# A fused RWKV-6 attention and GELU MLP on one core: the end of the first token tile put in another order, with two packing transfers in place of six

## The chip, the cores and the metric

The kernel runs on one NeuronCore of a Trainium2 chip. The metric is the device time of one execution in microseconds (us); the time shown is the median of the runs. Names of engines: PE is the matrix engine (PEld its weight loads), DVE the vector engine, ACT the scalar engine, POOL the general engine, SP the engine that here only issues transfers. ACT issues a few transfers as well.

## The reference

Four batch rows, 8 heads, 768 steps, head size 48. The recurrence of each head, followed by a two-layer MLP with exact GELU on all 3072 tokens:

```python
for t in range(S):
    cur = np.einsum('bhd,bhe->bhde', u[None] * kt, vt)
    y[:, :, t] = np.einsum('bhd,bhde->bhe', rt, state + cur)
    state = wt[:, :, :, None] * state + np.einsum('bhd,bhe->bhde', kt, vt)
x = attn_out.transpose(0, 2, 1, 3).reshape(3072, 384)
h = x @ w_in                                   # 384 x 2048
out = 0.5 * h * (1 + erf(h / sqrt(2))) @ w_out # 2048 x 384
```

The two weight matrices come as 64-bit floats and are made into 32-bit floats on the chip.

## The kernel before

**Tiles.** The 3072 tokens are cut into 8 tiles of 384 (half of one batch row). Tile x first goes through `attention(x, unit)`, which leaves the 384 x 384 activations transposed in `xT`, and then through `mlp(x)`, which reads `xT`. While PE works on the MLP of one tile, the attention of the next is woven into it. Only the first tile has no MLP to be woven into: its attention is all there is to do.

**Order.** Each piece of work is a Python generator, and the string `PLAN[x]` names, letter by letter, which generator goes on to its next `yield`. The order of the instructions on each engine is therefore written out by hand; engines run their own instructions strictly in that order and wait for each other through semaphores. For tile 0 the letters are: "." unit 0 and "s" unit 1 (the two halves of the heads, which go through `attention` one after the other, offset by a step), "f" the attention of tile 1, "c" the conversion of weights, "l" the loads of weights and of tile 1, "w" the values of tile 1, "x" the function `warm`. What is left of ".slxw" after the string is run out at its end.

**Attention of the first tile.** Inside a chunk of 64 steps the products of r and k are formed by levels (1, 2, 4, 8, 16, 32). For each level PE multiplies (`products`, L480), a part of the result goes to `a_sb`, and DVE multiplies r and k by the decays of the level (`update`, L522, or both at once, L533). At level 32 only the update of k is done at once; the one of r is kept in the list `last_r`, and the copies of the products to `a_sb` in `last_rows`. In this text the last products of the two units are called the last bursts. Then follow, for each unit:
- k is transposed on PE (`kt_ps`, L720, 6 transposes in two banks; there are just two such banks, tag "mm"), ACT copies it to `kx` (L727);
- the copies of `last_rows` (L738), on ACT for unit 1 and on DVE for unit 0; then r is updated by `last_r`;
- `kv_ps` (L764): the products of k and v for each chunk;
- `inside()` (L805): `y_ps`, what comes from inside the chunks;
- `chain_states` (L784, then 10 dependent instructions L779): the states of the chunks, one after the other, on DVE;
- `fences()` (L815, L817): DVE reads one element of `y_ps`, after which PE adds the states' share to it (L847);
- the output goes from `y_ps` to `xT`. A head has 48 rows and a column of `xT` has place for 64 in each half, so three of the four pairs of heads fill rows 0 to 47 of the halves (L854, L870), and the last pair is copied to `ysb` (L873) and laid into the free 16 rows of the three columns by transfers (L877), the packing transfers. For tile 0 three of these six go out from SP and three from ACT, for the other tiles all six from SP.

`x_rows` permutes the rows of `w_in` on the host to fit this layout.

**After it.** `mlp(0)` starts with `h_ps` (L1238): for each of 16 column blocks f of `w_in` three matmuls, one for each column j of `xT`. Before it stand the first products of tile 1 (L480), three matmuls on zeros (`keep_warm`, L253), and behind its first block the products of tile 1 that read ru = u * r (`kx`, made by ACT, L429).

**Weights.** A weight piece is 128 x 768 values in 64 bits. `prepare` makes two 32-bit parts of it by three ACT instructions (L361, L362, L364), `finish` puts them together on DVE (L373, L377). The pieces are prepared two ahead (`HALFWAY`), so the third piece, number 2, is prepared while piece 0 is finished. Loads of the first pieces and of tile 1 wait for a one-column memset on DVE (L191, L232), which sets when SP may issue them.

Of the kernel before, what the change touches and what calls it, by code (L numbers as in the profile page):

```python
# [22 lines left out]
G = 64  # L23
D = 48
# [12 lines left out]
NC_SP = 8  # L37
HALFWAY = 2
PLAN = {
    0: ".lls.....sslsc.lsslll.sl.sls..sl.lscsl..sss.lscs.lscs.s.ssssclll..s...sss..cs...sw.ccff",  # L40
    1: (
        ".cswc.ccc.cccss.lc.ccscs..cc.cs.cclwcsc.ccssc.c.cccsccc..ssccc.c.lcls.cc.ccsc.w.clwscclccc"
        ".c.swcw.ss.ccs.lcsc..cwcccslccslff..w..fw.wfs..f..flffffffww"
# [36 lines left out]
def kernel(  # L80
# [25 lines left out]
    nc = tc.nc  # L106
# [5 lines left out]
    NJ = DM // 128  # L112
# [183 lines left out]
    for i, h in enumerate(QUARTERS[:1]):  # L296
        for a in range(3):
            w_q = (3 - a) * C // 4
            z = q_ints[1 if a == 0 else 2]
# [35 lines left out]
    def conversion():  # L335

        i = converted[0]
        if i >= len(pieces):
            return
        converted[0] += 1  # L340

        prepare(i + HALFWAY)
        yield
        if wide:
            yield from finish(pieces[i][0], raws[i], *halfway[i])
        for _ in weight_in(i + 3):
            pass
# [5 lines left out]
    def prepare(upto):  # L353
        if not wide:
            return
        for i in range(len(halfway), min(upto, len(pieces))):
            words = raws[i].bitcast(U32).rearrange("p (a b) -> p a b", b=2)
            lo, hi = words[:, :, 0], words[:, :, 1]
            f = cv.tile([128, PIECE], U32, name="f")
            e = cv.tile([128, PIECE], U32, name="e")  # L360
            nc.scalar.activation(out=f.bitcast(F32), in_=hi.bitcast(F32), func=AF.Abs, scale=2.0 ** -112)  # L361
            nc.scalar.activation(out=e.bitcast(F32), in_=lo, func=AF.Identity, scale=2.0 ** -51, bias=two)  # L362
            sign = e.bitcast(F16).rearrange("p (a b) -> p a b", b=2)[:, :, 1]
            nc.scalar.activation(out=sign, in_=hi.bitcast(F32), func=AF.Copy, scale=2.0 ** -100)  # L364
            halfway.append((f, e))
# [15 lines left out]
    def attention(x, unit):  # L381
# [16 lines left out]
        xT = xT_of[x]  # L398
# [307 lines left out]
        last_r, last_rows = [], []  # L706
# [3 lines left out]
        if x < 2:  # L710
            kts = []
            for b in range(np_):
                if x == 0:
                    kt_ps = [ps.tile([128, BANK], F32, name="kt_ps", tag="mm", bufs=2) for _ in range(2)]
                else:
                    kt_ps = pair("kt_ps")
                    kt_ps = [kt_ps[:, z] for z in range(2)] + [kt_ps]
                for i in range(NI):
                    o = (i % N3) * 128
                    nc.tensor.transpose(kt_ps[i // N3][:, o:o + 128], k[:, (b * NI + i) * 128:(b * NI + i + 1) * 128], ident)  # L720
                if x == 0:
                    yield
                kt = kx[:, parts[b] * Q * T:(parts[b] + 1) * Q * T].rearrange("p (i g d) -> p i g d", g=2, d=G)
                kt2 = kt.rearrange("p (b i) g d -> p b (i g d)", b=2)
                if x == 0:
                    for z in range(2):
                        nc.scalar.copy(out=kt2[:, z], in_=kt_ps[z][:, 0:N3 * 128])  # L727
                else:
                    nc.scalar.copy(out=kt2, in_=kt_ps[2][:, :, 0:N3 * 128])
                kts.append(kt)  # L730

            if x == 0:
                yield
                for ah, d in last_rows:
                    for p in range(2):
                        rows = slice(p * 64, p * 64 + C // 2)
                        copy = nc.scalar.copy if unit else nc.vector.tensor_copy
                        copy(out=ah[rows, :, :, 0], in_=d[rows, :, :, 0])  # L738
                yield
                for z in last_r:  # L740
                    z()

            def k_t(b, i, p, g):
                return kts[b][half[p], i, g, :]
        else:

            for z in range(4):
                nc.scalar.copy(out=block_of_kt(z, z), in_=kb[z * 32:(z + 1) * 32, z])

            def k_t(b, i, p, g):  # L750
                return kt_q[half[p], g, b * NI + i]
# [23 lines left out]
        def chain_states(steps):  # L775
            for c in steps:
                if c or not first:
                    for q in range(qs):
                        nc.vector.scalar_tensor_tensor(out=stq[:, q, c], in0=stq[:, q, c - 1] if c else b4[:, q, NC - 1],  # L779
                                                       scalar=totq[:, q, c:c + 1], in1=kvs[q // Q][:, q % Q, c // 2, c % 2],  # L780
                                                       op0=ALU.mult, op1=ALU.add)
                else:
                    for b in range(np_):
                        nc.vector.tensor_copy(out=stq[:, b * Q:(b + 1) * Q, c], in_=kvs[b][:, :, 0, 0])  # L784
# [34 lines left out]
        if x == 0:  # L819

            inside()
            yield
            chain_states(range(NC - 1 + int(first)))
            yield
            fences()
            yield
        else:
            for c in range(0, NC, 2):
                chain_states(range(c, min(c + 2, NC - 1 + int(first))))
                if x > 1 and c + 2 < NC:  # L830
                    yield
            yield
            inside()
            fences()
            yield
# [23 lines left out]
        for b in reversed(range(np_)):  # L859
            for q in reversed(range(Q)):  # L860
                which = parts[b] * Q + q
                if x == 0 and which == NP - 2:

                    yield
                y = ys[b][1][:, :, q * N3 * C:(q + 1) * N3 * C].rearrange("p c (i t) -> p c i t", t=C)
                if which < NJ:
                    for z in range(2):
                        s = slice(z * G, z * G + D)
                        copy = nc.vector.tensor_copy if x == 0 else nc.scalar.copy
                        copy(out=xT[s, which, :].rearrange("p (i c t) -> p c i t", c=2, t=C), in_=y[s])  # L870
                    continue
                ysb = wk.tile([128, T], F32, name="ysb", bufs=1)
                nc.scalar.copy(out=ysb.rearrange("p (i c t) -> p c i t", c=2, t=C), in_=y)  # L873
                for z in range(2):
                    for j in range(NJ):
                        e = z * G + j * (G - D)
                        (nc.scalar if x == 0 and z * NJ + j > 2 else nc.sync).dma_start(out=xT[z * G + D:(z + 1) * G, j, :], in_=ysb[e:e + G - D, :])  # L877
        yield


# [500 lines left out]
    second = load_second(nc.sync)  # L1381

    def weights():
        prepare(1)
        yield
        while converted[0] < len(pieces):
            yield from conversion()
            yield

    def next_v():  # L1390
        load_v(1, nc.sync)
        yield

    def warm():
        for _ in range(1):
            keep_warm(3, True)
            yield

    def masks_and_sums():
        yield from make_quarter_masks()  # L1400
# [4 lines left out]
    for x in range(NX):  # L1405
        if x == 2:
            homes()
        following = attention(x + 1, 0) if x + 1 < NX else iter(())
        if x == 0:
            streams = {  # L1410
                ".": units[0], "s": units[1], "f": following, "c": pieces_of_w, "w": next_v(), "x": warm(),
                "l": chain(weight_in(0, True), islice(second, 5), weight_in(1, True), weight_in(2, True), second),
            }
        else:
            streams = {
                ".": mlp(x - 1), "s": slots, "f": following,
                "l": load(x + 1, nc.sync),
                "x": sums_of_x15(x) if x == NX - 1 else sums_of_x(x) if x > 1 else iter(()),
                "w": masks_and_sums() if x == 1 else chain(first_sum(), h_sums()) if x == 2 else sums_of_w15() if x == NX - 1 else iter(()),
                "c": pieces_of_w if x == 1 else iter(()),  # L1420
            }
        for c in PLAN[x]:
            next(streams[c], None)
        for c in ".slxw" if x == 0 else ".slxwc":
            while next(streams[c], streams) is not streams:
                pass
        slots = following
        if x == 1:
            fewer_pairs()
# [4 lines left out]
def x_rows(n_pairs):  # L1434

    rows = []
    for j in range(n_pairs - 1):
        for z in range(2):
            for p in range(G):
                q, e = (j, p) if p < D else (n_pairs - 1, j * (G - D) + p - D)  # L1440
                rows.append((2 * q + (z ^ q // Q % 2)) * D + e)
    return rows

# [48 lines left out]
```

## Time and profile before

| | |
|---|---|
| median of three runs | 591.1 us (587.8, 591.1, 591.87) |
| the profiled execution's own time | 593.53 us |
| its span, first to last instruction | 591.7 us |
| around the span | 1.8 us |
| mean granted PE clock | 0.997 |
| DVE busy, ACT busy | 463 us (78%), 276 us (47%) |
| PE busy from 0 to 50 us | 38.4 of 50 us |
| PE busy from 50 to 200 us | 150 of 150 us |

The profile shows one execution. A timeline line has the start in us, the duration, the engine, the line of the kernel, the operation with output and input, the number of instructions, and in brackets how long the engine stood idle before it and what ended that. A 32-bit matmul is recorded as two instructions. A q behind an engine's name means the engine's issuing side: "SPq L877" is SP issuing a transfer, "DMA xT<-ysb" the transfer itself until it has landed.

### The profile page before, as it was taken

What the parts mean: (1) busy time and instruction counts of PE and PEld (TensorE: products, weight loads), DVE (VectorE), ACT (ScalarE), POOL (GpSimd) and SP (SyncE); (2) the same over time, 40 slices, a digit from 0 to 9 for tenths busy, and PEclk for the clock granted to TensorE, in tenths of its full rate; (3) what the DMA queues carried; (4) which work ended last, traced back from release to release, by engine and by line L of the source; (5) the groups of instructions that cost most, each with busy time, mean ns of one, the idle gap of its engine ahead of it and who ended that gap; (6) DMA issues with size and microseconds to landing.
All of it is one profiled execution on the core that took longest, in us unless ns stands there. A gap on an engine that the chain in (4) does not pass through costs nothing.

```text
span 591.7 us, 17422 instructions
## 1 busy us (share of the span) xinstructions
PE 574.6 (97%) x7509; PEld 509.4 (86%) x7509; DVE 462.9 (78%) x907; ACT 276.0 (47%) x640; POOL 8.0 (1%) x21
## 2 busy tenths in 40 slices
PE   6789999999999999999999999999999999999998
PEld 3566666766799999999998999999999999989997
DVE  5879767988969986787859987688768998985532
ACT  2267889323612558046461468235561465523400
POOL 3100000000000000000000000000000000000000
PEclk9999999999999999999999999999999999999999
DMA  6549671020142311241022310420015200210000
GB/s 237 192 155 320 220 260 56 31 91 1 26 143 78 90 38 31 81 125 38 0 57 86 125 37 16 100 89 33 2 29 166 73 2 2 41 39 8 1 14 34
DMA packets 51004, 46.80 MB, mean 79 GB/s; under 512 B 31728, under 2 KB 36080, under 8 KB 50928
## 3 DMA queue, kind: packets, MB, share of 16 engines
q1 hardware_dynamic: 50832, 45.62, 25.3%
q8 instruction: 59, 0.97, 0.7%
q14 instruction: 17, 0.14, 0.1%
q10 hardware_dynamic: 96, 0.07, 0.1%
HBM read 36.24 MB, written 4.72 MB: 69 GB/s over the span
## 4 chain that ended last, share of the span: by engine, by line
PE 83%; DVE 8%; DMA 4%; SPq 3%; issue 1%; ACT 0%; DVEq 0%
PE o_ps L1252 25%; PE h_ps L1026 15%; PE u_ps L1026 12%; PE h_ps L1238 11%; PE d L619 4%; PE d L480 4%; PE o_ps L1332 4%; SPq L562 2%; PE c_ps L1026 2%; DVE st L779 2%; DMA rkw<-in_rkw_dram 2%; PE y_ps L805 2%; PE y_ps L847 2%; PE kv_ps L764 1%; DMA rkw<-kx 1%
## 5 line engine op out<-in xcount | busy, mean ns | idle before, releaser
L1026 PE MATMUL h_ps<-xT,w_in_sb 128*128 128x192 f32 x408 | 81.2, 330 | 0.1
L1026 PEld LDWEIGHTS h_ps<-xT,w_in_sb 128*128 128x128 f32 x408 | 67.8, 190 | 3.1 <-ACT g L1058 1.2
L1238 PE MATMUL h_ps<-xT,w_in_sb 128*128 128x384 f32 x192 | 64.4, 490 | 0.2 <-DMA xT<-ysb 0.2
L1238 PEld LDWEIGHTS h_ps<-xT,w_in_sb 128*128 128x128 f32 x192 | 35.8, 190 | 24.4 <-issue 0.8
L1252 PE MATMUL o_ps<-w_out_sb,g 128*128 128x192 f32 x224 | 39.5, 326 | 0.0
L1252 PEld LDWEIGHTS o_ps<-w_out_sb,g 128*128 128x128 f32 x224 | 36.9, 190 | 0.3
L480 PEld LDWEIGHTS d<-rkw 64*64 64x64 f32 x1152 | 21.2, 148 | 16.0 <-issue 11.2
L635 ACT COPY a_sb<-d 32x256 f32<-32x256 f32 (+8 forms) x90 | 32.6, 363 | 4.6 <-PE d L619 3.1
L1252 PE MATMUL o_ps<-w_out_sb,f 128*128 128x192 f32 x176 | 31.6, 329 | 0.0
L1252 PE MATMUL o_ps<-t,g 128*128 128x192 f32 x176 | 31.4, 329 | 0.0
L1252 PE MATMUL o_ps<-w_out_sb,e 128*128 128x192 f32 x176 | 31.4, 329 | 0.0
L1252 PE MATMUL o_ps<-t,e 128*128 128x192 f32 x176 | 31.2, 328 | 0.0
L1252 PE MATMUL o_ps<-t,s 128*128 128x192 f32 x176 | 30.9, 327 | 0.0
L480 PE MATMUL d<-rkw 64*64 64x64 f32 (+1 forms) x1152 | 23.8, 236 | 6.7 <-DMA rkw<-in_rkw_dram 3.5
L652 DVE COPY_PREDICATED a_sb<-quarter,d 128x480 f32<-128x480 uint8 (+5 forms) x54 | 23.2, 438 | 8.6 <-PE d L619 7.3
L779 DVE SCALAR_TENSOR_TENSOR st<-st,tot_sb,kv_ps 128x48 f32<-128x48 f32 x160 | 29.0, 257 | 1.0 <-PE kv_ps L764 0.8
L1026 PE MATMUL u_ps<-s,w_in_sb 128*128 128x192 f32 x160 | 29.5, 327 | 0.0
L1252 PEld LDWEIGHTS o_ps<-t,g 128*128 128x128 f32 x176 | 28.7, 190 | 0.4
L1252 PEld LDWEIGHTS o_ps<-w_out_sb,e 128*128 128x128 f32 x176 | 28.7, 190 | 0.3
L1252 PEld LDWEIGHTS o_ps<-w_out_sb,f 128*128 128x128 f32 x176 | 28.7, 190 | 0.3
L1252 PEld LDWEIGHTS o_ps<-t,e 128*128 128x128 f32 x176 | 28.8, 190 | 0.2
L1252 PEld LDWEIGHTS o_ps<-t,s 128*128 128x128 f32 x176 | 28.9, 190 | 0.1
(236 smaller groups left out, 1170.8 us busy)
## 6 DMA issues: line engine op xcount, KB each, us to landing
rkw<-in_rkw_dram SPq DMA_DIRECT2D x54, 256.0 KB, 4.1
raw<-in_w_out_dram SPq DMA_DIRECT2D x8, 768.0 KB, 5.0
v_in<-in_v_dram SPq DMA_DIRECT2D x8, 584.0 KB, 4.6
raw<-in_w_in_dram SPq DMA_DIRECT2D x5, 768.0 KB, 6.8
out_dram<-o_sb SPq DMA_DIRECT2D x20, 192.0 KB, 2.0
rkw<-kx SPq DMA_DIRECT2D x72, 48.0 KB, 2.0
rkw<-in_rkw_dram SPq DMA_DIRECT2D x6, 384.0 KB, 5.2
raw<-in_w_in_dram SPq DMA_DIRECT2D x9, 256.0 KB, 5.1
```

The source lines that it names most:

```text
L480: nc.tensor.matmul(d[half[p], g, n * width:(n + 1) * width], lhsT=kc[half[g], b, i, p], rhs=right(half[g], b, i, p), start=True, stop=True)
L562: dma.dma_start(out=block_of_kt(dst, src), in_=kb[src * 32:(src + 1) * 32, dst])
L619: nc.tensor.matmul(o[half[p], i * 3 * C // 2:(i + 1) * 3 * C // 2], lhsT=kc[half[g], n // NI, n % NI, p], rhs=rx[half[g], 2 * n + p], star ...
L635: nc.scalar.copy(out=at[z, g, first:behind, (a + 1) * h:], in_=d[z, :, :, to] if g == slice(None) else d[z, :, to])
L652: nc.vector.copy_predicated(out=an[:, :, :, :, (a + 1) * h:], mask=mask.to_broadcast(data.shape), data=data)
L779: nc.vector.scalar_tensor_tensor(out=stq[:, q, c], in0=stq[:, q, c - 1] if c else b4[:, q, NC - 1], scalar=totq[:, q, c:c + 1], in1=kvs[q ...
L805: nc.tensor.matmul(y[p][half[g ^ swap(b)], i * C:(i + 1) * C], lhsT=vs(b, i, g)[half[p]], rhs=at[half[p], g, b * NI + i, :], start=(i == 0 ...
L847: nc.tensor.matmul(ys[b][0][c % 2][half[g ^ swap(b)], i * C:(i + 1) * C], lhsT=src[half[g], o:o + G], rhs=rc[half[g], b, i, c % 2], start= ...
L1026: nc.tensor.matmul(o, lhsT=lhsT, rhs=rhs, start=start, stop=True, skip_group_check=True)
L1238: nc.tensor.matmul(h_ps, lhsT=w_in_sb[:, f // FI, j, f % FI * 128:(f % FI + 1) * 128], rhs=xT[:, j, :], start=(j == 0), stop=(j == NJ - 1))
L1252: nc.tensor.matmul(o, lhsT=lhs(j), rhs=rhs(j), start=start and j == 0, stop=(j == HF - 1), skip_group_check=True)
L1332: nc.tensor.matmul(o, lhsT=block(i, f // HF, f % HF), rhs=w_out_sb[:, f, :], start=(f == 0), stop=(f == NF - 1))
```

## The change

1. The string of tile 0 is changed in its second half. In the order of the instructions this puts the last bursts of both units next to each other, before the transposes of either; unit 0's transposes come right after unit 1's, and both `kv_ps` before either `y_ps`. The last instruction that finishes weight piece 0 (L377) comes two steps earlier on DVE, and the last third of piece 2's load goes out after the whole of piece 3's instead of before it.
2. `last_r` is run after `inside()`, ahead of `chain_states`, instead of before `kv_ps`.
3. The copies of `last_rows` change engines: DVE for unit 1, ACT for unit 0.
4. `prepare` has a yield before the third ACT instruction of piece 2; in the order of the instructions, this one comes after the copies of `y_ps` to `xT`.
5. The packing transfers of each half become one: two transfers of 16 x 3 x 384 values instead of six of 16 x 384. For tile 0 one goes out from SP and one from ACT. `x_rows` is changed to fit.
6. `warm` and its three matmuls are gone.

```diff
-    0: ".lls.....sslsc.lsslll.sl.sls..sl.lscsl..sss.lscs.lscs.s.ssssclll..s...sss..cs...sw.ccff",
+    0: ".lls.....sslsc.lsslll.sl.sls..sl.lscsl..sss.lscscc.lss.s...ss..s.llls.csssss....sw.cccff",
...
-        prepare(i + HALFWAY)
+        yield from prepare(i + HALFWAY)
...
             nc.scalar.activation(out=e.bitcast(F32), in_=lo, func=AF.Identity, scale=2.0 ** -51, bias=two)
+            if i == HALFWAY:
+                yield
...
-                        copy = nc.scalar.copy if unit else nc.vector.tensor_copy
+                        copy = nc.vector.tensor_copy if unit else nc.scalar.copy
                         copy(out=ah[rows, :, :, 0], in_=d[rows, :, :, 0])
-                yield
-                for z in last_r:
-                    z()
...
             inside()
+            yield
+            for z in last_r:
+                z()
             yield
             chain_states(range(NC - 1 + int(first)))
...
                 for z in range(2):
-                    for j in range(NJ):
-                        e = z * G + j * (G - D)
-                        (nc.scalar if x == 0 and z * NJ + j > 2 else nc.sync).dma_start(out=xT[z * G + D:(z + 1) * G, j, :], in_=ysb[e:e + G - D, :])
+                    (nc.scalar if x == 0 and z else nc.sync).dma_start(
+                        out=xT[z * G + D:(z + 1) * G, :, :].rearrange("p j t -> p (j t)"), in_=ysb[z * G:z * G + D, :])
...
-    def warm():
-        for _ in range(1):
-            keep_warm(3, True)
-            yield
...
-                q, e = (j, p) if p < D else (n_pairs - 1, j * (G - D) + p - D)
+                q, e = (j, p) if p < D else (n_pairs - 1, (p - D) * (n_pairs - 1) + j)
```

More of the change, by code (lines that the diff above doesn't have):

```diff
@@ L1383, in weights @@
     def weights():
-        prepare(1)
+        yield from prepare(1)
         yield
@@ L1410 @@
             streams = {
-                ".": units[0], "s": units[1], "f": following, "c": pieces_of_w, "w": next_v(), "x": warm(),
+                ".": units[0], "s": units[1], "f": following, "c": pieces_of_w, "w": next_v(),
                 "l": chain(weight_in(0, True), islice(second, 5), weight_in(1, True), weight_in(2, True), second),
@@ L1423 @@
             next(streams[c], None)
-        for c in ".slxw" if x == 0 else ".slxwc":
+        for c in ".slw" if x == 0 else ".slxwc":
             while next(streams[c], streams) is not streams:
```

## The prediction

> **What bounds the kernel.** I read the page's engine totals first: PE is busy 97% of the span. Then PE's waits after the first tile, from 48 us to the end:
>
> ```profile
> PE kv_ps L764 <- DMA rkw<-kx: 1.3, 2, 1.0
> PE y_ps L805 <- DVE st L779: 1.0, 3, 0.4
> PE y_ps L847 <- issue: 0.2, 1, 0.2
> PE h_ps L1238 <- DMA xT<-ysb: 0.2, 1, 0.2
> ```
>
> Each line gives total us, times, longest. In 540 us PE waits 2.7 us: from the first MLP on, PE sets the end, and the time moves by what the start of mlp(0) moves. So the chain of waits from 25 to 50 us is the view that matters (start, us, what):
>
> ```profile
> 33.49 0.57 DVE rkw L522
> ...
> 34.20 0.85 PE kt_ps L720 x6
> ...
> 37.00 0.56 DVE a_sb L738
> 37.55 0.03 issue
> 37.59 0.27 DVE st L784
> 37.85 0.03 issue
> 37.88 1.84 DVE st L779 x10
> 39.72 0.07 DVE fence L817
> ...
> 41.95 0.47 ACT ysb L873
> 42.42 0.02 issue
> 42.44 0.61 SPq L877
> ...
> 43.82 4.16 DMA xT<-ysb
> 47.97 0.14 issue
> 48.11 0.88 PE h_ps L1238 x2
> ```
>
> Unit 1's state chain on DVE could start at 37.59 only because DVE was copying unit 0's rows (L738); then come the chain, the states' share on PE, ysb, three transfers one behind the other on SP, and the third lands 4.16 us after its issue. PE's timeline shows how nearly it kept up with that:
>
> ```profile
> 42.90 1.38 PE L847 MATMUL y_ps<-rkw,st 64*64 64x64 f32 x40 [0.32 <-DVE fence L815]
> 44.12 1.73 PE L480 MATMUL d<-rkw 64*64 64x32 f32 x96
> 45.78 0.82 PE L253 MATMUL warm<-zeros 128*128 128x512 bf16 x3
> 46.44 1.45 PE L1238 MATMUL h_ps<-xT,w_in_sb 128*128 128x384 f32 x4
> 48.11 0.88 PE L1238 MATMUL h_ps<-xT,w_in_sb 128*128 128x384 f32 x2 [0.21 <-DMA xT<-ysb]
> ```
>
> My mark is the end of that first block, where tile 1's next products start: 48.92.
>
> **Bursts, transposes, r.** Up to unit 1's last burst (32.50) PE's order is the same. Unit 0's burst follows it: its r and k are ready at 33.07 (L533, 32.11 + 0.96), so it runs 33.24 to 34.17, in what was PE's 0.77 us wait for the update of k. Unit 1's transposes still start at 34.20. Unit 0's now come right behind, but there are two banks, so they wait for ACT's copies of unit 1's (34.75 to 35.61): a new wait. Behind it on PE stands unit 1's kv_ps, and DVE's chain waits for that: transposes end about 36.1, kv_ps runs 36.08 to 36.95 (before: to 36.59, so 0.36 later). DVE meanwhile does both updates of k (to 34.8), the copies of unit 1's rows (1.11, to 35.9) and r (0.56, to 36.6), all ahead of 36.95; L377 (0.95) has moved into DVE's idle 1.35 us before 32.11 and costs nothing, and the memsets behind it release their loads about 0.6 to 0.9 us later. Those loads have room: the last of them were moved by 39.4 (the transfer engines fall to 0.06 busy at 40), the first products of tile 1 want theirs at 43.5. So the chain starts at 37.0 instead of 37.59: 0.58 us gained.
>
> From there the same steps follow in the same order: chain and fence (2.2), states' share of unit 1, inside of unit 0, fence, states' share of unit 0, tile 1's products. Unit 1's `inside` (37.75 to 38.7, behind ACT's new row copies) is done before its fence at 39.2, as is r. PE's unexplained 0.40 us inside L847 (at 40.17, "issue") sits at the same count of instructions, and I keep it; nearest other such pauses are 0.71 and 1.76 us, so this is -0.4 to +1.4, and I take 0. Everything moves by 0.58: ysb ends at 41.85, tile 1's products end where h_ps can start, at 45.2.
>
> **Warm-up removed.** 46.44 - 45.78 = 0.66 us of PE's path.
>
> **Transfers.** SP and ACT issue one each at 41.9. Before, the first column needed two transfers and only the third column waited; now the first matmul waits for both. Needed at 45.2, they may take 3.3 us. What is shown for old ones, for tile 0:
>
> ```profile
> DMA to landing us min/median/max: 1.9/2.0/4.2
> ```
>
> The first on SP took 2.1, with an empty queue before it, as now. The two new ones carry 147 KB; the first old pair's 48 KB moved in some 0.35 us (the bytes seen from 43.6 to 43.9), so three times as much adds 0.7: landing after 2.8 us (an estimate from these rows), at 44.7, with 0.5 us to spare. The upper bound is the row of the third old one, 4.16, which had the load of v on its heels, issued 0.88 us after it; now that load follows again, some 0.7 us behind. I take 2.8: nothing stands in front of it on SP (idle 5.6 us), and the load's bytes came about 1.2 us after its issue, so at 43.8 to 44.0, as the packing ends. On that queue the later transfers (v, two weight pieces, tile 2) all go 2 us earlier.
>
> [...]
>
> The old wait for the third column is gone: six matmul records at 0.33 us (7.94 us for 24) are 1.98, so the block would have ended at 48.6 without it, against 48.92: 0.35 us with warm-up's overlap. Sum: 45.2 + 1.98 = 47.2 against 48.92, or -1.7 (0.58 + 0.66 + 0.35, and 0.1 of rounding).
>
> **Third weight piece in two parts.** L364 (1.07) now stands behind the copies to xT, ahead of ACT's L429, on which the products after the first block wait. ACT's copies start at 43.85, L364 at 44.75, the four L429 end at 46.3, 46.8, 47.35 and 47.9 (0.53 each); their products want them from 47.2 in steps of 0.4: no wait, 0.3 us if all starts faster. Before, the piece was ready at 40.82 and ACT idled 1.11 before ysb, so taking it off that path gains nothing. Its DVE half was wanted at 50.5 and PE's at 56.4: room.
>
> **Later tiles.** In each, four issues on SP fall away (0.59 each); only h_ps and DVE's sums wait for them, and PE showed no such wait. From 0 to -1.3 (all waits of kv_ps for transfers), and I take 0. Pieces of w_in and w_out come with at least 3 us of room (piece 1 ready at 49.5, used at 52.4; the last of w_out ready at 107.5, used at 111.2), and ACT, nearly full at 90 to 100 us, last waited for PE at 81.1, so it moves with PE.
>
> **Rivals.** (1) The packing lands behind the load of v, 4.16 us after issue, at 46.1: the block ends at 48.1, -0.85, so 590.25. For it: that very row, and its equal order. Against: the first transfer's 2.1. (2) The clock: PE had 1.94 us of work in 24 to 28 us, and then this came:
>
> ```profile
> 28.00:31.00 3.00, 2.79 (x62) 1.84 (x66) 2.54 (x7) 2.85 (x4) 0.00 (x0) 0.55 0.20 52
> ```
>
> The third number from the right is the granted clock, 0.55. If leaving out the three matmuls brought that on again for 3 us at the start of h_ps, 3 x 0.45 = 1.35 us would be lost: -0.35, so 590.75. Against: from 39 to 41 us PE did 0.76 us of work in 2 us and was granted 1.00. [...] (3) Slower: the packing transfers get caught in the burst of loads that now starts 2 us earlier. A load of tile 2 issued at 47.9 took 7.5 us to land; at that price h_ps starts at 41.9 + 7.5 = 49.4 and the block ends at 51.4, +2.5, so 593.6. It decides from a landing of 5.0 us (41.9 + 5.0 + 1.98 = 48.9). For it: transfers up to 394 GB/s from 50 us; against: all of those loads are issued after the packing. (4) PE's gain is given back because weights or loads stay where they are: 591.1. Against: the room above. (5) SP's emptier queue also ends the 1.3 us waits of kv_ps: -3.0, so 588.1. Against: other issues stand between, for tiles 2 and 3.
>
> **The numbers.** Forecast -1.7: the profiled execution of 593.53 (span 591.7 and 1.8 around it) would be 591.8, span 590.0. The median of the runs is 2.4 below that execution, and from it I get 589.4. Chances: forecast 0.50, (1) 0.22, (2) 0.06, (3) 0.08, (4) 0.08, (5) 0.06. The range goes from (5) to (2), 588.1 to 590.75, and 1.0 us beyond on both sides, because three runs that lie 4.1 us apart do not fix a median better (an estimate): 587.1 to 591.75. About what a measurement can tell from no change is 1%, 5.9 us: no case reaches it. What is left is scatter of the runs: faster 0.03, slower 0.04, within 0.93.
>
> **What would show it.** Right: the first L784 near 37.0, h_ps starting about 45.2 with no wait, the products after it near 47.2, and PE without waits after that. Rival (1): h_ps starts near 46.1 with a wait for xT<-ysb. Rival (2): a granted clock under 1.00 between 44 and 50. Rival (3): a wait there of over 3.5 us. The prediction is wrong if PE shows new waits after 48 us, or if the first chain does not start earlier.

## The result, and the profile after

| | before | changed |
|---|---|---|
| median | 590.67 us (587.8 to 591.87, 8 runs) | 594.91 us (592.64 to 599.19, 8 runs) |
| ratio, 95% interval | 1 | 1.0081, 1.0057 to 1.0106 |
| profiled execution, its span | 593.53, 591.7 us | 597.55, 595.8 us |
| mean granted PE clock | 0.997 | 0.991 |

The kernel became 0.8% slower, about 4 us, where 1.7 us less was forecast; 594.91 lies outside the range of 587.1 to 591.75. PE is still busy 97% of the span.

PE's waits from 48 us to the end, of the changed kernel (total us, times, longest):

```profile
PE d L482 <- issue: 1.9, 1, 1.9
PE y_ps L804 <- DVE st L778: 1.1, 3, 0.4
PE h_ps L1027 <- DVE o_sb L1376: 0.7, 1, 0.7
PE kv_ps L763 <- DMA rkw<-kx: 0.7, 2, 0.5
```

The wait for `xT<-ysb` is gone, as intended. At the top stands something new: 1.9 us in one piece, put down to "issue", which means that nothing the profile shows held PE. PE's timeline shows where:

```profile
39.32 1.98 PE L849 MATMUL y_ps<-rkw,st 64*64 64x64 f32 x33 [1.83 <-issue]
...
43.20 2.16 PE L849 MATMUL y_ps<-rkw,st 64*64 64x64 f32 x38 [0.32 <-DVE fence L814]
45.15 0.25 PE L482 MATMUL d<-rkw 64*64 64x32 f32 x2
...
46.80 2.17 PE L1239 MATMUL h_ps<-xT,w_in_sb 128*128 128x384 f32 x6
48.90 0.68 PE L482 MATMUL d<-kx,rkw 64*64 64x64 f32 x27
51.50 1.87 PE L482 MATMUL d<-kx,rkw 64*64 64x64 f32 x69 [1.92 <-issue]
53.30 9.00 PE L1239 MATMUL h_ps<-xT,w_in_sb 128*128 128x384 f32 x24
62.23 1.60 PE L482 MATMUL d<-rkw 64*64 64x32 f32 x96
```

The same place before:

```profile
48.92 1.63 PE L480 MATMUL d<-kx,rkw 64*64 64x64 f32 x96
50.48 8.01 PE L1238 MATMUL h_ps<-xT,w_in_sb 128*128 128x384 f32 x24
58.42 1.60 PE L480 MATMUL d<-rkw 64*64 64x32 f32 x96
```

The first block of h_ps starts without a wait right behind tile 1's products. Then PE stops after 27 of 96 records of the products that read kx, and no wait for an operand is shown. The 24 records of h_ps after it take 9.00 us (before: 8.01), and the last 38 of L849 2.16 us (before: 1.38 for 40). The windows say why (width, then busy us of PE, PEld, DVE, ACT and POOL, then granted clock, share of the transfer engines, GB/s):

```profile
40.00:44.00 4.00, 3.68 (x93) 3.50 (x91) 1.06 (x4) 0.48 (x1) 0.00 (x0) 0.50 0.12 33
...
48.00:52.00 4.00, 2.08 (x62) 1.26 (x64) 3.66 (x12) 3.42 (x8) 0.00 (x0) 0.99 1.05 398
52.00:56.00 4.00, 4.00 (x56) 2.73 (x49) 3.77 (x4) 1.57 (x2) 0.00 (x0) 0.58 1.01 372
```

Over the 4 us after each stop the granted clock was 0.50 and 0.58; before, it was 1.00 from 40 to 56 us. And while PE stands at 50 us, the transfer engines are full (a share of 1.05 from 48 to 52 us).

From tile 1's first products to the end of the 24 h_ps, before took 14.30 us (44.12 to 58.42) and the changed kernel 17.08 (45.15 to 62.23). The 2.78 us between are: the block of h_ps starts sooner and waits less, -1.05; the stop, +1.92; the rest of those products, most of them on the slow clock, +0.92; h_ps on the slow clock, +0.99. From the end of those 24 h_ps to the end of the span it is 533.3 us before and 533.6 in the changed kernel (531.6 to 533.6 in all profiles of ordinary length, of both kernels and of the experiments). So all but 0.3 of the 4.1 us between the two spans arises in the first 62 us.

The remaining 1.03 us lie ahead of tile 1's first products, and there the two executions are no even match. At unit 1's last burst the changed kernel stood 3.16 us ahead (29.34 against 32.50), because before had shortly ahead of it stopped for 1.76 us and run on a clock of 0.55. It lost that lead and 1.03 us more up to 45.15, behind its stop of 1.83 us inside L849 (0.40 in L847 before) and the slow clock after it.

### The profile page after: what moved, and what is told of

Its sections match the earlier page's. It is cut to its first block, busy times and chain, and to the rows that moved or that the text cites. A ratio compares the mean times of both kernels' runs of the same rounds, so it can differ in the third digit from the quotient of the medians.

```text
span 595.8 us, 17357 instructions
## 1 busy us (share of the span) xinstructions
PE 577.1 (97%) x7506; PEld 511.9 (86%) x7506; DVE 462.7 (78%) x907; ACT 275.7 (46%) x640; POOL 8.0 (1%) x21
## 5 line engine op out<-in xcount | busy, mean ns | idle before, releaser
L1242 ACT ACTIVATE g<-h_ps 128x256 f32<-128x256 f32 (+1 forms) x32 | 13.9, 434 | 31.1 <-PE h_ps L1239 30.5
```

The source lines that it names most:

```text
L1242: nc.scalar.activation(out=gs[group][:, f % FG, 0:t], in_=h_ps[:, 0:t], func=AF.Gelu)
```

## What the stops are: a theory and its rivals

The page's list of DMA queues has a row that I had not used (packets, MB, share):

```profile
q1 hardware_dynamic: 50352, 45.62, 25.0%
q8 instruction: 59, 0.97, 0.7%
```

One packet of q8 is 0.97 MB / 59 = 16 KB. PE has 7506 matmuls and 7506 weight loads; in 59 pieces that is 254 instructions each, some 64 bytes apiece (estimates from these rows). And the stops on PE stand at multiples of 128 matmul records: between the two shown, 38 of L849, 48 of L804, 40 of L849, 96 of the tile's products, 6 of h_ps and 27 make 255, two pieces less one record. From this I take it that PE's own program comes in pieces of 128 matmuls and their weight loads during the run, over the transfer engines that carry the data (q1 25.0% of them, q8 0.7%).

When a piece moved is seen by cutting the run into slices of 0.4 us and looking for the packet. For the piece that the products of kx need, from 48.8 to 49.2 us of the changed kernel:

```profile
q1 hardware_dynamic: 83, 0.16, 104.2%
q8 instruction: 1, 0.02, 15.7%
```

Before, the same piece moved between 45.2 and 45.6 us, 1.1 to 1.5 us after PE had entered the piece ahead of it (44.12), beside little else:

```profile
q1 hardware_dynamic: 29, 0.02, 23.6%
q8 instruction: 1, 0.02, 20.7%
```

Now it moved 3.7 us or more after that point (45.15). What came in between is on SP's timeline (start, time of issue):

```profile
42.16 0.69 SPq L877 DMA_DIRECT2D xT<-ysb  x1
42.98 0.49 SPq L184 DMA_DIRECT2D v_in<-in_v_dram  x1
43.52 1.01 SPq L228 DMA_DIRECT2D raw<-in_w_in_dram  x2
44.78 0.53 SPq L204 DMA_DIRECT2D rkw<-in_rkw_dram  x1
45.41 2.55 SPq L228 DMA_DIRECT2D raw<-in_w_in_dram  x2
```

Before, v was issued only after PE had entered the piece at 44.12, and the loads behind it later still:

```profile
44.70 0.61 SPq L184 DMA_DIRECT2D v_in<-in_v_dram  x1
45.35 2.42 SPq L228 DMA_DIRECT2D raw<-in_w_in_dram  x2
```

With two packing transfers SP is free sooner: v and three large loads were issued from 42.98 on, before PE entered the piece at 45.15, and from 44 to 48 us the transfer engines were busy for a share of 0.98 (before: 0.58).

The theory: the loads, issued ahead of PE's code, delay it; PE stands, and a long stand can bring its clock down (to the 0.50 and 0.58 above). It is theory 1 or T1 in the expectations, which call a stop a pause. The rivals: the missing warm-up lets the clock fall (theory 2, T2 below); the two transfers cost the time by themselves, by landing too late (theory 3); the new order of the work costs the time by itself.

## The experiments

**Six transfers again.** The changed kernel with the old packing (and the old `x_rows`):

```diff
-                    (nc.scalar if x == 0 and z else nc.sync).dma_start(
-                        out=xT[z * G + D:(z + 1) * G, :, :].rearrange("p j t -> p (j t)"), in_=ysb[z * G:z * G + D, :])
+                    for j in range(NJ):
+                        e = z * G + j * (G - D)
+                        (nc.scalar if x == 0 and z * NJ + j > 2 else nc.sync).dma_start(out=xT[z * G + D:(z + 1) * G, j, :], in_=ysb[e:e + G - D, :])
```

> The changed kernel with the six old packing transfers, all else as changed. Theory 1 (PE's code comes through the transfer engines, and with fewer issues on SP the load of v and the weights start ahead of it): SP starts those loads some 1.3 us later, the pause of 1.9 us inside the products of tile 1 that read kx shrinks below 0.5 us, the one inside L849 stays near 1.8; 590.5 to 593. Theory 2 (the three warm-up matmuls are missing, the PE clock falls): pauses and time stay, 594 to 596. Theory 3 (the two larger packing transfers are worse by themselves, in every tile): about 590.7, with the waits for xT in all tiles differing.

Measured: 591.20 us, ratio 1.0021 (0.9997 to 1.0046). No stop in the products of kx, and h_ps waits 0.66 us for `xT<-ysb` instead; the stop inside L849 stays, at 1.82. Most of the loss hangs on the packing.

**Two transfers alone.** The kernel before with the edit above the other way round and nothing else.

> The kernel before with nothing but the two packing transfers in place of six (and the matching row order of w_in). Theory 1: v and the weights are loaded 1.3 us earlier against PE's position, PE's code for the first products of tile 1 comes later, a pause of 0.5 to 2 us near 44 to 50 us; 591 to 594. Theory 2: the warm-up matmuls are there, so 590 to 591. Theory 3: 593 to 595.

Measured: 592.19 us, 1.0027 (1.0004 to 1.0050). v is issued at 42.59, ahead of PE's entry at 44.01; the code moves between 48.0 and 48.4, and the products of kx stop for 1.57 us. So the stop comes with the two transfers in the old order too. In this profile it is shorter, and h_ps behind it ran as fast as in before (8.01 us for 24).

**The code shifted.** 64 matmuls of 16 columns on zeros, behind the warm-up at the start; no operand, transfer or wait is touched:

```diff
     keep_warm(8)
+    shift = ps.tile([128, BANK], F32, name="warm", tag="mm", bufs=2)
+    for _ in range(64):
+        nc.tensor.matmul(shift[:, 0:16], lhsT=zeros[:, 0:128], rhs=zeros[:, 0:16], start=True, stop=True)
```

> The changed kernel with 64 tiny matmuls on zeros (16 columns) more in the first idle stretch of PE, before anything has landed. They cost no time there, but every later PE instruction stands 128 places later in its code. Theory 1: the pauses named issue come 64 matmuls earlier in the program than before (none 2 records into L849, none 27 records into the products that read kx), their sum after 30 us changes by more than 1 us, and the time moves by 1 to 4 us, most likely down to 591 to 594. Theories 2 and 3: pauses stay where they are and the time stays at 594 to 596.

Measured: 597.41 us, 1.0103 (1.0048 to 1.0157). The stops moved to places 64 records away, 0.77 us behind 66 records of tile 1's products and 1.79 us behind 91 of those that read kx. That the stops follow the count of instructions is shown. The time did not fall to 591 to 594, the likeliest of the expected values; from four runs it can't be told from the changed kernel's 1.0081. The same with 50 matmuls:

> The changed kernel with 50 tiny matmuls on zeros in PE's first idle stretch. Code comes in stretches of 128 matmuls, so the place of the pause in the products that read kx (27 matmuls in) moves 78 matmuls on, to 9 matmuls into the second group of h_ps, where a stretch lasts 6.7 us instead of 3.5 because h_ps takes 0.33 us a matmul; the one in L849 moves into unit 0's inside products. Theory 1: no pause over 0.5 us from 42 us on, the sum after 30 us under 1.2; 589 to 592.5, clearly under the changed kernel (594.9), with not one transfer or dependence changed. If the code has nothing to do with it: 594 to 596.

Measured: 592.86 us, 1.0023 (1.0000 to 1.0047) against the changed kernel's 1.0081, by an edit that adds work and moves no transfer in the program. One stop of 0.80 us stands at 43.8 us, where none over 0.5 was expected; from 46 us on none over 0.5 us is left. If the order or the landing of the transfers cost the time, this edit could not give it back.

**v held back, a first try.** A one-column clear on DVE between its copies to xT (L872 and L856), which the load of v must wait for; in the PLAN it stands at the old place of `w`:

```diff
     def next_v():
-        load_v(1, nc.sync)
+        loaded[1][1] = io.tile([128, v.shape[2]], F32, name="v_in", bufs=1)
+        nc.vector.memset(loaded[1][1][:, 0:1], 0.0)
+        nc.sync.dma_start(out=loaded[1][1], in_=v[1])
         yield
```

> The changed kernel, where the load of tile 1's v waits for a one-column memset on DVE behind the copies of unit 1's output to xT, so SP issues it and all loads behind it about 1.3 us later. Theory 1: the pause inside the products that read kx falls from 1.9 to under 0.7 us, 591 to 593.5. Theories 2 and 3: no change, 594 to 596.

Measured: 592.17 us, 1.0036 (1.0019 to 1.0053). The clear ran at 43.16, v was issued at 43.29, and PE entered the piece at 43.35: held too little. The code moved at about 46.6, and the stop was 1.11 us, where under 0.7 was expected.

**Held further, with other loads.** The same clear one step later, and the last three loads of tile 1 (L192) later too: the tail of PLAN[0] from `.llls.csssss....sw.cccff` to `.s.cssslllss....s.wcccff`.

> The changed kernel with its bulk loads held back until PE's code has been fetched: the last three loads of tile 1 go out behind unit 1's state chain (near 37 us) instead of at 33.6, and the load of tile 1's v, with all behind it on SP, behind the last copies of unit 0 to xT (near 45 us). No other instruction moves. Theory 1 (code behind loads): the pause inside L849 falls from 1.8 to under 0.5, the one in the products that read kx from 1.9 to under 0.5, the clock stays over 0.9 from 33 us on; 587.5 to 590, under the kernel before. Theory 2 (missing warm-up matmuls): the idle time in L849 and the time stay, 594 to 596. Theory 3 (packing transfers worse by themselves): 594 to 596.

Measured: 592.28 us, 1.0023 (0.9999 to 1.0047), and not the 587.5 to 590 that was expected. The one execution that was profiled took 2048.32 us and is left out; a second profile:

> The changed kernel with its bulk loads held back, once more, for its profile. Theory 1 as it stands: no pause over 0.5 us in L849 nor in the products that read kx, and what keeps it above 590 us is another wait between 37 and 60 us, of DVE or ACT for the later loads. If the pauses are still there, the loads that were held back are not what the code waits for.

Measured: 591.11 us in this one execution, span 589.3 (the median of the kernel before, measured beside it, was 590.48). v at 42.99, PE's entry at 41.48; the stop in the products of kx is 0.21, the one inside L849 0.15, and the clock is 1.00 from 18 to 56 us; 0.98 us appear at the boundary one piece earlier. The stops went as expected, and yet no time was gained.

**The warm-up back.** The changed kernel with the three matmuls of `warm()` in front of h_ps.

> The changed kernel with the three warm-up matmuls back before the first h_ps. Theory 1: their own 0.66 us is added and the pauses stay: 594 to 596.5. Theory 2: the clock stays at 1.00 through the first h_ps, 590.5 to 592.

Measured: 595.19 us, 1.0071 (1.0042 to 1.0101). T2 falls. Its profiled execution is one of the short ones (592.09 us, where the runs go from 590.81 to 596.91) and had no stop in those products, though v was issued (42.41) before PE's entry (43.41): the order of the two makes the stop likely, not certain.

**No warm-up, nothing else.** The kernel before without `warm()`.

> The kernel before without the three warm-up matmuls, nothing else. My prediction: up to 0.66 us faster. Theory 1: the first h_ps then waits for the third packing transfer of SP instead, so -0.3 to 0: 590.0 to 591. Theory 2 (they hold the clock): slower, 592 to 594.

Measured: 590.89 us, 1.0012 (0.9989 to 1.0034). No gain and no loss that can be told; a gain of the whole 0.66 us (0.9989) lies at the very edge of the interval.

**The order alone.** The changed kernel with six transfers and the warm-up.

> The kernel before with the new order of the first tile's end alone (letters, r, row copies, third piece in two parts): six transfers, warm-up kept. My prediction: 0.58 us faster than before, 589.5 to 590.3. Theory 1: the order moves the chain little, because unit 0's last burst waits for ACT's copies; 590 to 591.5.

Measured: 592.78 us, 1.0034 (1.0013 to 1.0056); one of its twelve executions took 606.62 us and does not enter the ratio. The new order gains nothing and costs about 2 us, more than either expectation had, without a stop in the products of kx.

**Both kernels once more**, for a second profile.

> The kernel before once more, for a second profile: do its pauses repeat? Theory 1: none over 0.5 us in the products that read kx, since the load of v goes out after PE has passed into its last 128 instructions before them; the one in L847 anywhere from 0.4 to 2 us. 588 to 592.

> The changed kernel once more, for a second profile. Theory 1: pauses of 1.5 to 2.2 us both in L849 and in the products that read kx, and a granted clock below 0.9 behind at least one of them. 593 to 598.

Measured: before 590.63 (span 588.8), no stop in the products of kx. Changed 594.66 (span 592.8): no stop inside L849, 2.32 us in the products of kx, and h_ps behind it 9.58 us for 24. So the stop inside L849 comes and goes (before_again has 2.09 us at kv_ps and 0.59 in L847); the stop at kx stayed.

**v alone held back far enough.** The clear of gate_v, and one letter of the PLAN moved: `sw.cccff` to `s.wcccff`.

> The changed kernel as it is, with one thing put in: DVE clears one column of tile 1's v behind its last copies to xT, so that SP can issue the load of v, and the four loads behind it, only then; no other transfer and nothing on PE is moved. T1 (the loads that now stand ahead of PE's code for the products that read kx delay it): v is issued at least 0.5 us after PE's first products of tile 1 start, the pause in the products that read kx falls from 1.9 to 2.3 us to under 0.4, and the time to 0.998 to 1.003 of the kernel before. If the loads are not the cause: the pause stays over 1 us, and the time at 1.006 to 1.010; it then also pays for the later loads. If only the clock were the cause, the pause may go but the products of the first MLP stay slow (24 of h_ps over 8.5 us).

Measured: 591.93 us, 1.0016 (0.9999 to 1.0033). SP's and PE's timelines and the slice from 44.4 to 44.8 us:

```profile
41.67 0.69 SPq L877 DMA_DIRECT2D xT<-ysb  x1
45.27 0.33 SPq L1394 DMA_DIRECT2D v_in<-in_v_dram  x1
```

```profile
43.65 0.25 PE L482 MATMUL d<-rkw 64*64 64x32 f32 x2
...
45.29 2.17 PE L1239 MATMUL h_ps<-xT,w_in_sb 128*128 128x384 f32 x6
47.40 1.63 PE L482 MATMUL d<-kx,rkw 64*64 64x64 f32 x96
48.95 8.01 PE L1239 MATMUL h_ps<-xT,w_in_sb 128*128 128x384 f32 x24
56.89 1.60 PE L482 MATMUL d<-rkw 64*64 64x32 f32 x96
```

```profile
q8 instruction: 1, 0.02, 15.0%
```

PE enters at 43.65, the code moves within 1.15 us, v follows at 45.27, all 96 products run in one piece, and h_ps runs at the speed of before (8.01 us for 24, at a clock of 1.00 from 48 to 56 us). The stop inside L849, ahead of all this, stays (1.82). The same stretch as above is 13.24 us (43.65 to 56.89), 1.06 less than before. Holding v, and with it the loads behind it, back took the ratio from 1.0081 to 1.0016; v now follows the packing's issue by 3.60 us, in the changed kernel by 0.82.

**The two transfers, held, in the old order.** `two_only` with the same hold.

> The kernel before with the two packing transfers alone, and the same hold of the load of v. T1: two_only had a pause of 1.57 us in the products that read kx and 1.0027; with the hold the pause is under 0.4 and the time 0.996 to 1.001. If the packing in two transfers costs something else (a later landing of xT): h_ps waits for xT<-ysb and the time stays at 1.002 to 1.004. If the wait for the old third transfer was worth anything on the path, this version would be under 0.999, which would beat both kernels.

Measured: 590.76 us, 0.9998 (0.9976 to 1.0020). PE enters at 43.77, v is issued at 45.39, no stop at kx, h_ps without a wait. The rival of the late landing falls: packed in two, xT is in time. But no gain can be told either.

Thirteen profiles side by side, all but the one left out and those of the two shifted codes, whose boundaries lie elsewhere (us; "PE enters" is the start of tile 1's first products, "moved" is known to some 0.2 us):

| profile | PE enters | v issued | code moved | stop at kx |
|---|---|---|---|---|
| before | 44.12 | 44.70 | 45.4 | 0 |
| before_again | 42.04 | 42.43 | 43.2 | 0 |
| six_transfers | 42.09 | 42.49 | 43.0 | 0 |
| nowarm_only | 42.61 | 42.80 | 43.4 | 0 |
| order_only | 44.55 | 44.94 | 45.6 | 0 |
| late_again | 41.48 | 42.99 | 43.8 | 0.21 |
| hold_v | 43.65 | 45.27 | 44.6 | 0 |
| two_hold | 43.77 | 45.39 | 44.6 | 0 |
| gate_v | 43.35 | 43.29 | 46.6 | 1.11 |
| warm_back | 43.41 | 42.41 | 46.0 | 0 |
| two_only | 44.01 | 42.59 | 48.2 | 1.57 |
| changed | 45.15 | 42.98 | 49.0 | 1.92 |
| after_again | 42.41 | 41.51 | 46.8 | 2.32 |

Where v comes after PE's entry, the code moves 0.8 to 2.3 us after that entry; where v comes first, 2.6 to 4.4 us.

## Why the prediction was wrong, point by point

**Transfers: "On that queue the later transfers (v, two weight pieces, tile 2) all go 2 us earlier."** This sentence is the cause, and it was costed at nothing. I had asked whether those loads would catch the packing (the first and third rivals) and not what else travels on the same engines. The packing was in time in hold_v, two_hold and both profiles of the changed kernel; neither rival came. PE's code was caught instead: 1.9 to 2.3 us of stop, and 1.0 to 1.6 us more in h_ps behind it, in the changed kernel's profile on a clock of 0.50. A new wait of PE after 48 us was also the sign of being wrong that the prediction had named.

**"PE's unexplained 0.40 us inside L847 ... I take 0."** The row was there, with 0.71 and 1.76 beside it, all called "issue". They are stops of one kind: from 0.71 to 1.76 it is 128 records, from there to 0.40 it is 382, three pieces less two records. The bound of +1.4 that I gave was for one stop at that place, and the profiled execution of the changed kernel reached it there (1.83 against 0.40). The stop that decided the medians came at another boundary, where before had none.

**Bursts, transposes, r: -0.58.** Wrong in sign; order_only, which has the third weight piece in two parts with it, measures +0.34% (0.13 to 0.56). The step left out a wait. Unit 0's burst was put right behind unit 1's "in what was PE's 0.77 us wait"; it waits for ACT's copies at L546, as after_again shows, first on PE and then on ACT:

```profile
29.96 0.93 PE L482 MATMUL d<-rkw 64*64 64x64 f32 x48
32.29 0.93 PE L482 MATMUL d<-rkw 64*64 64x64 f32 x48 [1.40 <-ACT a_sb L546]
```

```profile
28.18 0.93 ACT L361 ACTIVATE f<-raw 128x768 f32<-128x768 f32 x1 [6.43 <-DMA raw<-in_w_in_dram]
29.00 1.00 ACT L362 ACTIVATE e<-raw,two 128x768 f32<-128x768 uint32 x1
30.04 1.08 ACT L366 ACTIVATE e<-raw 128x768 f16<-128x768 f32 x1
30.99 2.55 ACT L546 COPY a_sb<-d 16x192 f32<-16x192 f32 x8
```

ACT does a weight piece first, and has waited 6.43 us for that piece to land; half of the eight copies are done at 32.27, and the burst starts. In after_again, six_transfers, late_again and hold_v this burst starts 4.11 to 4.15 us after L361, whatever PE does; the wait is 0.46 to 1.40 us, and both units' transposes and kv_ps now stand behind it. In the profile of before PE came so late to the place (last burst at 32.50, after a stop of 1.76 us and a slow clock) that ACT was ready: with those times the forecast of 33.24 holds, but the one execution was no measure of where ACT and PE meet. From unit 1's last burst to tile 1's first products after_again took 12.45 us, before 11.62 with its stop of 0.40: longer by 1.2, not shorter by 0.6.

That wait is not the whole price of the order. In the profile of order_only PE came late to the place (after a stop of 2.31 us), ACT was ready, and yet the burst started 1.33 us after unit 1's (32.29 against 30.96) instead of the forecast's 0.74. It waited 0.40 us for DVE, on which L379, the moved L377 of before, stood in front of the update that the burst reads:

```profile
30.31 0.95 DVE L379 CUSTOM_DVE_ANT_0 w_in_sb<-f,e 128x1536 uint16<-128x1536 uint16 x1
30.96 0.93 PE L482 MATMUL d<-rkw 64*64 64x64 f32 x48
31.19 0.95 DVE L535 TENSOR_TENSOR rkw<-rkw,tot_sb 128x768 f32<-128x768 f32 x1
32.29 0.93 PE L482 MATMUL d<-rkw 64*64 64x64 f32 x48 [0.40 <-DVE rkw L535]
```

So "L377 (0.95) has moved into DVE's idle 1.35 us ... and costs nothing" was wrong too: that idle time belonged to an execution in which PE had a slow clock (0.55 from 28 to 31 us). The stop inside L849 may come on top: 1.55 to 2.10 us in six of the eight profiles of the new order that the table has, against 0 to 1.59 in L847 in the five of the old (two of which, before_again and nowarm_only, have 2.09 and 2.20 at kv_ps). How the price divides among these was not tested.

**Warm-up and the old wait: -0.66 and -0.35.** Right where they stand: from tile 1's first products to those of kx before took 4.80 us (44.12 to 48.92), after_again 3.85, the changed kernel 3.75. They did not reach the end. The profile of nowarm_only has 4.12 us there, yet over 12 runs no gain can be told; whether it drowns in the scatter of the stops or is given back at them is not shown.

**Rival (2), the clock.** The clock did fall, to 0.50 for some 3.4 us (51.9 to 55.3), longer than the 3 us I gave it; but it followed PE's stand, and the warm-up put back did not help (warm_back 1.0071). Slower had got a chance of 0.04, and by more than 1% the median is not slower; the forecast of -1.7 and the range were wrong all the same.

**Right:** PE sets the end. The two transfers land in time, 2.7 and 3.2 us after their issue (I had estimated 2.8, and 3.3 were allowed). In hold_v, where v is far behind, it is 2.6 and 3.1, so v on their heels cost them about 0.1 us. In the changed kernel v took 4.2 us from its issue at 42.98: the packing did not land behind it, as the first rival had it. L364's two halves and the later tiles' fewer issues show no wait that is new: the 0.7 us of h_ps for o_sb in the first list stands in before_again too.

Open: the six versions of the new order in which the stop at kx is gone or shorter (six_transfers, gate_v, late_loads, shift_50, order_only, hold_v) lie 0.16 to 0.36% above before, and the intervals of two of them, gate_v and order_only, lie above it as a whole; the price of the order is thus known to some 0.2%. Stops of 1.11 and 1.57 us at kx (gate_v, two_only) left h_ps at 8.01 us for 24, those of 1.92 and 2.32 us took it to 9.00 and 9.58. The length alone does not decide, though: behind a stop of 2.10 us inside L849 the clock of gate_v stayed at 1.00. No version beats the kernel before.

## What to carry to other kernels

A stop called "issue" at multiples of 128 matmuls was here, by the theory that held, PE waiting for its own program (1.11 to 2.32 us at kx); look for that pattern first. Before loads are moved ahead, see in the list of queues when the next packet of code moves, and try letting bulk loads start after it: an order that frees a queue sooner cost more here than it saved (1.0081, and 1.0016 with v held back). And where an instruction is pulled forward on one engine, look up what the engine that feeds it was waiting for; one execution does not tell where two engines meet.

## What was not expected of the hardware

- A piece of code needs time even when nothing large is ahead of it: in before PE enters at 44.12, and the packet moves at 45.4. In the changed kernel the packet moves at 49.0 and PE goes on at 51.50, 2.5 us later; in two_only 2.2 us later. The sum is some 3.5 us from PE's entry (an estimate from these rows). Among the small products before 30 us a piece lasted 4.16 us in before (20.62 to 24.78) and 4.52 us in the changed kernel (24.63 to 29.15), with stops of 1.76 and 0.19 us behind them: by the estimate, little room.
- PE was busy 2.08 of 4 us from 48 to 52 us in the changed kernel and was granted 0.58 over the next 4. But gate_v had only 0.94 of 4 (36 to 40 us) and kept 1.00 there and in the next 4. So with a stop of 1.92 us the clock fell, and with one of 2.10 us it did not.
- What the length of a stop leaves open, its place in time may settle. Cut into slices of 0.2 us, the clock goes to 0.50 at 38.26 and 51.92 in the changed kernel and is back at 45.10 and 55.33; before, it goes down at 28.30 and is back at 31.71 (estimates from the clock of these slices). The changes within the changed kernel's execution lie 6.84, 6.82 and 3.41 us apart, those within before's 3.41. In two_only, two_hold and shift_code the clocks of 4 us windows come to a fall of 3.4 us each (estimates, taking the clock as either 1.00 or 0.50). Counted in steps of 3.41 us, the last step ahead of a fall had PE busy for 1.68 and 1.49 us in the changed kernel and for 1.25 in before. Busy time is not all of it: in before one of 1.48 (4.40 to 7.82) passed without a fall. That a stop which lies across two steps may pass where one inside a single step does not is my guess; no run was made to test it.
- One execution of late_loads took 2048.32 us (a span of 2046.5), at a granted clock shown as 1.00. From 40 to 44 us PE was busy for all 4.00 us with 54 matmul records; in late_again it was busy for 2.76 with 130, at 1.00 as well.
